# Recurrence and routed experts on one core: moving the tiles that TensorE reads to multiples of 64 bytes

## The chip, the core and the metric

The kernel runs on one core of a Trainium2 chip. A core has five engines with a queue each: TensorE (PE, with its weight loads as PEld), VectorE (DVE), ScalarE (ACT), GpSimd (POOL) and SyncE (SP, which issues most DMAs). The metric is the device time of one execution in microseconds; the median of several runs is compared.

## The reference

Two steps. First a linear recurrence over 768 time steps, for 4 batches and 8 heads of width 48:

```python
for t in range(S):
    cur = einsum('bhd,bhe->bhde', u * k[t], v[t])
    y[:, :, t] = einsum('bhd,bhde->bhe', r[t], state + cur)
    state = w[t][..., None] * state + einsum('bhd,bhe->bhde', k[t], v[t])
```

Then its output, as 3072 rows of 384 values, goes through a mixture of 8 experts. Each row is sent to the one expert with the largest logit (`x @ w_gate` plus a bias by the row's modality), and the result is

```python
out[mask] = gate_w[mask, None] * (np.maximum(x[mask] @ w1[e], 0) @ w2[e])
```

with 1024 hidden values per expert. Inputs and output are float32.

## The kernel before

**Recurrence** (`att_iter`, 24 chunks of 128 time steps). VectorE makes running products of the decays with two scans (tiles B and E, lines 286 and 289), VectorE and GpSimd form R = r * E, K = k * B and G = r * k, and TensorE does the chunk's matmuls in float32, which shows in the profile as two passes: the transpose of K (line 313), the scores (337), the bonus term with G (268), the state's update (351), and the output from state (363) and from scores (375, 378). The output rows go to `xp`, are transposed (419) and multiplied with the gate's weights (425). Routing then gives each row a place, and an indirect DMA per 128 rows (`scatter`, line 624) writes 386 values of each, the row, its weight and its number, to a buffer in DRAM sorted by expert.

**Experts**. Six blocks of up to 512 sorted rows (the last has 416), and one small block of 128. In a block, `rows_load` reads the rows, `blk_t` turns them and splits each value into a float32r part xh and a rest xo. `blk_up` computes 8 tiles of 128 hidden values, each as 9 matmuls: 3 slices of the row times the three products (wh, xh), (wh, xo) and (wl, xh), where wh and wl are the same split of w1 (line 692). The moving operand is xh or xo, 512 columns; the stationary one is a 128x128 piece of wh or wl. ScalarE and VectorE turn the sum into hh and hl, again such a split (lines 695 and 696). `blk_down` uses hh and hl as stationary operands and rows of w2's split as moving ones, 384 columns: 8 x 4 x 3 = 96 matmuls a block (line 706). The small block does its up-projection in plain float32 (line 737) and its down-projection like the others (line 750). For each expert ScalarE and GpSimd or VectorE split the next weights in slices (lines 219 and 220).

**What sets the order.** It is written by hand: the loops at the end of the function issue every instruction in its place, and each engine takes its own in that order. Waits between engines come from semaphores that the framework sets for tiles that are written and read.

**What sets the addresses.** Tiles come from pools, which lie in SBUF from the left side upwards (weights `raw`, `wh`, `wl`, small constants, `rt` with xp of the second part, `xa`, `wk`, and after the recurrence `wp` and `bp`) and from the right side downwards (`mp` with xl, xg, xh, xo, xt; `pa` with the recurrence's inputs; `hp` with hh and hl). A tile begins at the next multiple of 32 bytes in each partition. So a tile's place behind a multiple of 64 depends on the sizes of those before it.

The lines that the change touches are the tiles of lines 81, 283 and 284, 399, 642 and 643, and the reads at 234 and 625.

Of the kernel before, what the change touches and what calls it, by code (L numbers as in the profile page):

```python
# [9 lines left out]
F32 = mybir.dt.float32  # L10
# [4 lines left out]
ALU = mybir.AluOpType  # L15
AX = mybir.AxisListType

B, H, S, D = 4, 8, 768, 48
P = 128
# [4 lines left out]
E, F = 8, 1024  # L24
KC = DM // P
FC = F // P
XW = DM + 2
# [3 lines left out]
JT = BT // P  # L31
# [13 lines left out]
XROWS = DUMMY + BT  # L45
PAD_ID = 1 << 20
W_LO, W_HI = 0.78, 1.25
TINY = 1e-16
NWARM = 12
NG = 8  # L50
CUT = (0, 10, NU)
NJS = (CUT[1], NU - CUT[1])
GW = B * H * S * D // (P * NG)
WHALF = FC // 2 * DM
# [3 lines left out]
def kernel(ctx: ExitStack, tc: tile.TileContext, rkw, vt, wf, cst, mid, wg, bias, w1, w2, out):  # L58
    nc = tc.nc
    ctx.enter_context(tc.manual_schedule())  # L60
    cp = ctx.enter_context(tc.tile_pool(name="cp", bufs=1, side="left"))
# [2 lines left out]
    xs = dp.tile([XROWS, XW], F32, name="xs")  # L64


    raw = [cp.tile([P, FC, DM], F32, name=f"raw{k}") for k in range(2)]
    wh, wl = ([cp.tile([P, FC, DM], F32R, name=f"{nm}0")] for nm in ("wh", "wl"))

# [3 lines left out]
    rt = ctx.enter_context(tc.tile_pool(name="rt", bufs=2, side="left"))  # L73
    xa = att.enter_context(tc.tile_pool(name="xa", bufs=1, side="left"))
    wk = att.enter_context(tc.tile_pool(name="wk", bufs=2, side="left"))
    bp = {"m": ctx.enter_context(tc.tile_pool(name="mp", bufs=1, side="right"))}
    pa = prep.enter_context(tc.tile_pool(name="pa", bufs=2, side="right"))
    PREP = ("B", "E", "K", "G")
    WORK = ("R", "KT", "A", "dT", "v")
    NIN = 4  # L80
    ins = [pa.tile([P, 1541], F32, name=f"in{i}", bufs=1) for i in range(NIN)]
    T = {}

    def wt(n, tag, sh, bufs=None, dt=F32):
        T[tag, n] = (pa if tag in PREP else wk if tag in WORK else rt).tile(sh, dt, tag=tag, name=f"{tag}{n}", bufs=bufs)
        return T[tag, n]

    def pt(n, tag, sh=(P, 512)):
        T[tag, n] = banks.get(tag, ps).tile(list(sh), F32, tag=tag, name=f"{tag}_{n}")
        return T[tag, n]  # L90
# [31 lines left out]
    wp = pt("w", "pR")  # L122

    def warm(n):

        for i in range(n):
            nc.tensor.matmul(out=wp, lhsT=wm[:, 0:P], rhs=wm, start=(i == 0), stop=(i == n - 1))

    warm(NWARM)
    d1s = cp.tile([P, 518], BF16, name="d1s")  # L130
# [9 lines left out]
    bb = cp.tile([P, 2 * E], F32, name="bb")  # L140
    mi = cp.tile([NU, 2 * P], I32, name="mi")

    SPb = []
    for i in range(3):
        t = wk.tile([P, 4, 2, D], F32, name=f"SPb{i}", bufs=1)
        SPb.append(t)
    vz = [wk.tile([P, 2, 2, 2, D], F32, name=f"vz{i}", bufs=1) for i in range(2)]
    gacc = cp.tile([P, 2 * NG], F32, name="gacc")
    glo = cp.tile([P, 1], F32, name="glo")
# [81 lines left out]
        nc.scalar.copy(out=T["pX", a], in_=quarters(src))  # L231

    def mk_r(a):
        nc.vector.tensor_tensor(out=wt(a, "R", [P, 4, P], 3), in0=T["pX", a], in1=quarters(T["E", a])[:, :, 0:P], op=ALU.mult)

    def mk_k(a, k):
        nc.gpsimd.tensor_tensor(out=wt(a, "K", [P, 4, P]), in0=quarters(k), in1=quarters(T["B", a][:, 1:517])[:, :, 1:129], op=ALU.mult)  # L237
# [17 lines left out]
    def quarters(v):  # L255
        return v.rearrange("p (a b) -> p a b", a=4)
# [4 lines left out]
    def ok(n):  # L261
        return 0 <= n < NU
# [15 lines left out]
    def att_iter(i):  # L278
        a, m, z = i + 2, i + 1, i
        if ok(a):  # L280
            t = ins[a % NIN]
            r, k, w = t[:, 0:512], t[:, 512:1024], t[:, 1024:1541]
            Bt = wt(a, "B", [P, 517])
            Et = wt(a, "E", [P, 516], 1)

            nc.vector.tensor_tensor_scan(out=Bt[:, 516:0:-1], data0=w[:, 516:0:-1], data1=d1[:, 516:0:-1],  # L286
                                         initial=0.0, op0=ALU.mult, op1=ALU.max)
            nc.vector.reciprocal(out=w[:, 0:516:129], in_=Bt[:, 1:517:129])
            nc.vector.tensor_tensor_scan(out=Et, data0=w[:, 0:516], data1=d1[:, 1:2].to_broadcast([P, 516]),  # L289
                                         initial=1.0, op0=ALU.mult, op1=ALU.max)  # L290
        if ok(z):
            dV = wt(z, "dV", [P, H, D], 2)
            nc.gpsimd.tensor_tensor(out=dV, in0=T["v", z][:, 0:DM].rearrange("p (a b) -> p a b", a=H),
                                    in1=T["dT", z].rearrange("p a b -> p (a b)")[:, :, None].to_broadcast([P, H, D]), op=ALU.mult)
# [10 lines left out]
        if ok(m):  # L305
            K, R, v = T["K", m], T["R", m], T["v", m]

            if i == 0:
                warm(NWARM // 2)
            if not last:  # L310
# [10 lines left out]
        if ok(m):  # L321
            A = wt(m, "A", [P, 2, 2, 3, 64])
            pS = pt(m, "pS", (P, 2, 512))[:, :, 0:384].rearrange("p a (b c d) -> p a b c d", b=2, c=3)
            for g in range(2):
                for s0, c in ((0, 0), (1, 64)):
                    for sw in range(2):
                        for hh in range(2):
                            q = slice(64 * hh, 64 * hh + 64)
                            o = slice(64 * (s0 ^ sw), 64 * (s0 ^ sw) + 64)
                            p = 2 * g + sw  # L330
                            if s0:
                                out, rhs = pS[o, hh, g, 1 + sw], R[q, p, 64:P]
                            elif sw:
                                out, rhs = pS[o, hh, g, 0:3:2], R[q, p].rearrange("p (a b) -> p a b", a=2)
                            else:
                                out, rhs = pS[o, hh, g, 0:2], R[q, p].rearrange("p (a b) -> p a b", a=2)
# [21 lines left out]
        if ok(z):  # L358
            A, R, v, pY = T["A", z], T["R", z], T["v", z], pt(z, "pY")
# [35 lines left out]
    def x_rows(n, by_two=False):  # L395
        c, j = part(n)
        if j == 0:

            T["xp", c] = (rt if c else xa).tile([P, NJS[c], XW], F32, tag="xp", name=f"xp{c}", bufs=1)
        if n == 0:  # L400
            T["R"] = pt("x", "pR")

            nc.tensor.matmul(out=T["R"][:, 511:512], lhsT=wm[:, 0:P], rhs=wm[:, 0:1], start=True, stop=True, skip_group_check=True)
        x, dV = T["xp", c][:, j, 0:DM], T["dV", n].rearrange("p a b -> p (a b)")
        if by_two:
            nc.scalar.copy(out=x, in_=T["pY", n][:, 0:DM])
            nc.gpsimd.tensor_tensor(out=x, in0=x, in1=dV, op=ALU.add)
        else:
            nc.vector.tensor_tensor(out=x, in0=T["pY", n][:, 0:DM], in1=dV, op=ALU.add)

    def part(n):
        c = n >= CUT[1]
        return int(c), n - CUT[c]
# [208 lines left out]
    def scatter(n):  # L622
        b, j = part(n)
        rows_apart("xs", nc.gpsimd.indirect_dma_start(out=xs[:, :], out_offset=bass.IndirectOffsetOnAxis(ap=posT[:, n:n + 1], axis=0),  # L624
                                     in_=T["xp", b][:, j, :], in_offset=None, bounds_check=XROWS - 1, oob_is_err=False))


    X = {}
# [1 line left out]
    def width(q):  # L630
        return BQ if q == NQ - 1 else BT
# [8 lines left out]

    def rows_load(q, at, nj):
        xl = bp["m"].tile([P, NXB, XC], F32, tag="xl", name=f"xl{q}", bufs=2)
        xg = bp["m"].tile([P, JT, 2], F32, tag="xg", name=f"xg{q}", bufs=4)
        r = nc.sync.value_load(e0r[0:1, 0:1] if q == 0 else tab[0:1, 1, ds(at, 1)], min_val=0, max_val=DUMMY)
        src = xs[ds(r, nj * P), :]
        if q == 0:
            nc.sync.dma_start(out=xl.rearrange("p a c -> p (a c)").rearrange("p (j c) -> p j c", j=JT),
                              in_=src[:, 0:DM].rearrange("(j p) c -> p j c", p=P))
        for i in range(4 if q else 0):
            nc.sync.dma_start(out=xl[32 * i:32 * i + 32, 0:4 * nj], in_=src[:, XC * i:XC * i + XC].rearrange("(b t) c -> t b c", t=32))  # L650
        nc.sync.dma_start(out=xg[:, 0:nj], in_=src[:, DM:XW].rearrange("(j p) c -> p j c", p=P))
        X["xl", q], X["xg", q] = xl, xg
# [7 lines left out]
    def blk_t(q):  # L660
        w = width(q)
        X["x", q] = [bp["m"].tile([P, KC, BT], dt, tag=nm, name=f"{nm}{q}", bufs=1) for nm, dt in (("xh", F32R), ("xo", F32R), ("xt", F32))]
        xg = X["xg", q]
        xh, xo, xt = ([t[:, m, 0:w] for m in range(KC)] for t in X["x", q])
        if q == 0:
            xl = X["xl", q].rearrange("p a c -> p (a c)").rearrange("p (j k m) -> p j m k", j=JT, m=KC)
            xt = [pt(f"x0_{m}", t) for m, t in enumerate(("pX", "pK", "pU"))]
            for m in range(KC):
                for j in range(JT):
                    nc.tensor.transpose(out=xt[m][:, j * P:(j + 1) * P], in_=xl[:, j, m], identity=ident)  # L670

        def rest(m):
            nc.vector.tensor_tensor(out=xo[m], in0=xt[m], in1=xh[m].bitcast(F32), op=ALU.subtract)

        for m in range(KC):
            if q:
                rows_turn(q, m, w // 32, xt[m])
            nc.scalar.copy(out=xh[m], in_=xt[m])
            if m:
                rest(m - 1)  # L680
        rest(KC - 1)
        nc.vector.reciprocal(out=xg[:, :, 0:1], in_=xg[:, :, 0:1])
# [97 lines left out]
    for i in range(-2, NU):  # L780
# [39 lines left out]
        if i == NU - 3:  # L820
# [5 lines left out]
                                       in_=zt[:, None, :].to_broadcast([P, JT, XW])))  # L826
# [4 lines left out]
    banks.update(pS0=pse, pS1=pse)  # L831
    bp["h"] = ctx.enter_context(tc.tile_pool(name="hp", bufs=1, side="right"))
    wp = ctx.enter_context(tc.tile_pool(name="wp", bufs=1, side="left"))
    for w, nm in ((wh, "wh"), (wl, "wl")):
        w.append(wp.tile([P, FC, DM], F32R, name=f"{nm}1"))
    bp["p"] = ctx.enter_context(tc.tile_pool(name="bp", bufs=1, side="left"))
# [4 lines left out]
    def tend(s):  # L841
        for n in range(NG):
            if s == 26 + 6 * n:
# [218 lines left out]
def _layout(inp):  # L1062
# [14 lines left out]
    for hh in range(2):  # L1077
# [15 lines left out]
        "vt": vt,  # L1093
        "wf": np.ascontiguousarray(w).reshape(P, NG * GW),
        "cst": c,
# [19 lines left out]
```

## Time and profile before

| | us |
|---|---|
| median of 3 runs | 345.57 |
| their range | 343.74 to 351.85 |
| profiled execution | 348.94 |
| its span | 347.20 |

| engine | busy, us | share of the span | instructions |
|---|---|---|---|
| PE | 331.1 | 95% | 3950 |
| PEld | 297.7 | 86% | 3951 |
| DVE | 211.3 | 61% | 368 |
| ACT | 203.5 | 59% | 461 |
| POOL | 196.9 | 57% | 222 |

The mean granted clock of TensorE is 0.995 of full. Busy time counts a stretch once, however many instructions overlap in it; since the end of a matmul is modelled, its start tells more than its duration.

### The profile page before, as it was taken

What the parts mean: (1) busy time and instruction counts of PE and PEld (TensorE: products, weight loads), DVE (VectorE), ACT (ScalarE), POOL (GpSimd) and SP (SyncE); (2) the same over time, 40 slices, a digit from 0 to 9 for tenths busy, and PEclk for the clock granted to TensorE, in tenths of its full rate; (3) what the DMA queues carried; (4) which work ended last, traced back from release to release, by engine and by line L of the source; (5) the groups of instructions that cost most, each with busy time, mean ns of one, the idle gap of its engine ahead of it and who ended that gap; (6) DMA issues with size and microseconds to landing.
All of it is one profiled execution on the core that took longest, in us unless ns stands there. A gap on an engine that the chain in (4) does not pass through costs nothing. (4 is left out here: it accounts for less than half of the span.)

```text
span 347.2 us, 10131 instructions
## 1 busy us (share of the span) xinstructions
PE 331.1 (95%) x3950; PEld 297.7 (86%) x3951; DVE 211.3 (61%) x368; ACT 203.5 (59%) x461; POOL 196.9 (57%) x222
## 2 busy tenths in 40 slices
PE   7899989999999979999999999999999999999993
PEld 3789889988888867899889988997899889999893
DVE  6999989999998545776333955933560454053010
ACT  3897989778587735641522667628745855632140
POOL 8989898689998723586650680246024503440462
PEclk9999999999999989999999999999999999999999
DMA  7997988877997322515537047026544762260011
GB/s 258 408 354 232 293 275 240 275 251 248 278 312 231 111 72 93 91 68 197 216 119 156 0 96 226 0 70 144 197 159 160 208 223 93 92 206 3 0 47 55
DMA packets 35587, 58.66 MB, mean 169 GB/s; under 512 B 17298, under 2 KB 22090, under 8 KB 35529
## 3 DMA queue, kind: packets, MB, share of 16 engines
q1 hardware_dynamic: 32424, 48.45, 45.7%
q0 software_dynamic: 3104, 9.47, 7.6%
q8 instruction: 33, 0.54, 0.6%
q14 instruction: 26, 0.20, 0.2%
HBM read 57.86 MB, written 12.67 MB: 203 GB/s over the span
## 5 line engine op out<-in xcount | busy, mean ns | idle before, releaser
L220 POOL TENSOR_TENSOR wl<-raw,wh 128x768 fp32r<-128x768 f32 x24 | 46.3, 1935 | 106.8 <-ACT wh L219 106.7
L219 ACT CAST wh<-raw 128x768 fp32r<-128x768 f32 x48 | 39.3, 832 | 42.5 <-PE pU_d L706 39.0
L696 DVE SCALAR_TENSOR_TENSOR hl<-pS_u,hh 128x512 fp32r<-128x512 f32 (+1 forms) x34 | 22.8, 675 | 44.0 <-ACT hh L695 44.0
L692 PE MATMUL pS_u<-xh,wh 128*128 128x512 f32 (+1 forms) x102 | 40.5, 397 | 0.4 <-DVE hl L696 0.4
L692 PE MATMUL pS_u<-xo,wh 128*128 128x512 f32 (+1 forms) x102 | 39.6, 389 | 0.0
L692 PE MATMUL pS_u<-xh,wl 128*128 128x512 f32 (+1 forms) x102 | 39.6, 388 | 0.0
L695 ACT ACTIVATE hh<-pS_u 128x512 fp32r<-128x512 f32 (+1 forms) x34 | 19.7, 586 | 33.0 <-PE pS_u L692 27.7
L237 POOL TENSOR_TENSOR K<-in,B 128x512 f32<-128x512 f32 x24 | 28.4, 1185 | 7.2 <-issue 2.7
L297 POOL TENSOR_TENSOR G<-in 128x512 f32<-128x512 f32 x24 | 30.8, 1284 | 0.0
L624 POOL DMA_INDIRECT xs<-xp,posT x24 | 26.2, 1092 | 7.3 <-issue 5.1
L286 DVE TENSOR_TENSOR_SCAN B<-in,pX_d 128x516 f32<-128x516 f32 x24 | 29.3, 1219 | 1.6 <-DMA in<-rkw 1.6
L220 DVE TENSOR_TENSOR wl<-raw,wh 128x768 fp32r<-128x768 f32 x24 | 27.2, 1141 | 4.9 <-ACT wh L219 4.6
L289 DVE TENSOR_TENSOR_SCAN E<-in,pX_d 128x516 f32<-128x516 f32 x24 | 29.5, 1229 | 0.8
L715 POOL DMA_INDIRECT out<-ot,xg x24 | 23.5, 979 | 9.1 <-issue 4.1
L378 PE MATMUL pY<-v,A 128*64 128x48 f32 x384 | 27.2, 225 | 1.3 <-issue 1.3
L378 PEld LDWEIGHTS pY<-v,A 128*64 128x64 f32 x384 | 25.7, 142 | 1.4 <-issue 1.4
L339 DVE TENSOR_TENSOR A<-pS,m 128x768 f32<-128x768 f32 x24 | 22.8, 949 | 3.3 <-PE pS L337 3.0
L696 DVE SCALAR_TENSOR_TENSOR hl<-pT_u,hh 128x512 fp32r<-128x512 f32 (+1 forms) x14 | 9.4, 668 | 25.3 <-ACT hh L695 25.3
L243 ACT ACTIVATE pU_st<-pU_st,B 128x48 f32<-128x48 f32 x80 | 22.0, 275 | 2.9 <-PE pU_st L351 0.5
L692 PEld LDWEIGHTS pS_u<-xh,wh 128*128 128x128 f32 x102 | 19.2, 188 | 4.5 <-DVE hl L696 0.8
L692 PEld LDWEIGHTS pS_u<-xh,wl 128*128 128x128 f32 x102 | 19.1, 188 | 4.2
L692 PEld LDWEIGHTS pS_u<-xo,wh 128*128 128x128 f32 x102 | 19.2, 188 | 3.6
(232 smaller groups left out, 911.3 us busy)
## 6 DMA issues: line engine op xcount, KB each, us to landing
raw<-w SPq DMA_DIRECT2D x24, 768.0 KB
in<-rkw SPq DMA_DIRECT2D x23, 512.0 KB
v<-vt SPq DMA_DIRECT2D x24, 288.0 KB
in<-rkw SPq DMA_DIRECT2D x23, 258.5 KB
wg<-wf SPq DMA_DIRECT2D x8, 576.0 KB
xl<-xs SPq DMA_DIRECT2D x20, 192.0 KB
raw<-w SPq DMA_DIRECT2D x16, 192.0 KB
xs<-zt SPq DMA_DIRECT2D x12, 193.0 KB
```

Source lines behind the costliest of these rows:

```text
L219: nc.scalar.copy(out=wh[k][:, sl], in_=raw[k][:, sl])
L220: (eng or (nc.vector, nc.gpsimd)[k]).tensor_tensor(out=wl[k][:, sl], in0=raw[k][:, sl], in1=wh[k][:, sl].bitcast(F32), op=ALU.subtract)
L237: nc.gpsimd.tensor_tensor(out=wt(a, "K", [P, 4, P]), in0=quarters(k), in1=quarters(T["B", a][:, 1:517])[:, :, 1:129], op=ALU.mult)
L286: nc.vector.tensor_tensor_scan(out=Bt[:, 516:0:-1], data0=w[:, 516:0:-1], data1=d1[:, 516:0:-1], initial=0.0, op0=ALU.mult, op1=ALU.max)
L289: nc.vector.tensor_tensor_scan(out=Et, data0=w[:, 0:516], data1=d1[:, 1:2].to_broadcast([P, 516]), initial=1.0, op0=ALU.mult, op1=ALU.max)
L297: nc.gpsimd.tensor_tensor(out=wt(a, "G", [P, 512]), in0=r, in1=k, op=ALU.mult)
L339: nc.vector.tensor_tensor(out=fl(A), in0=fl(pS), in1=m3.rearrange("p c d -> p (c d)")[:, None, None, :].to_broadcast([P, 2, 2, 192]), op=A ...
L378: nc.tensor.matmul(out=yh[64:P, g, sw, hh], lhsT=A[:, hh, g, 1 + sw], rhs=vs[:, g, hh] if sw else v[:, h * D:(h + 1) * D], start=new and n ...
L624: rows_apart("xs", nc.gpsimd.indirect_dma_start(out=xs[:, :], out_offset=bass.IndirectOffsetOnAxis(ap=posT[:, n:n + 1], axis=0), in_=T["xp ...
L692: nc.tensor.matmul(out=pp, lhsT=wsrc[0][:, f, c * P:(c + 1) * P], rhs=xsrc[:, c], start=(n == 0), stop=(n == 3 * KC - 1))
L696: nc.vector.scalar_tensor_tensor(out=hl, in0=pp, scalar=0.0, in1=hh.bitcast(F32), op0=ALU.max, op1=ALU.subtract)
L715: ins = nc.gpsimd.indirect_dma_start(out=out[:, :], out_offset=bass.IndirectOffsetOnAxis(ap=xg[0:n, j, 1:2].bitcast(I32), axis=0), in_=ot[ ...
```

## The change

It adds four tiles that nothing reads or writes (`pad0` to `pad3`) and makes some rows longer than what is used of them: the input tiles have 1600 values a row instead of 1541, B and E 576 instead of 517 and 516, xp 400 instead of 386, xg 4 instead of 2. What is read and written of each tile is as before, and so is every instruction and its place on its engine.

```diff
+PADW, PADK = 48, 80
...
+    cp.tile([P, 32], F32, name="pad0")
     raw = [cp.tile([P, FC, DM], F32, name=f"raw{k}") for k in range(2)]
...
-    ins = [pa.tile([P, 1541], F32, name=f"in{i}", bufs=1) for i in range(NIN)]
+    ins = [pa.tile([P, 1600], F32, name=f"in{i}", bufs=1) for i in range(NIN)]
...
+    wk.tile([P, PADK], F32, name="pad3", bufs=1)
     SPb = []
...
-        nc.vector.tensor_tensor(out=wt(a, "R", [P, 4, P], 3), in0=T["pX", a], in1=quarters(T["E", a])[:, :, 0:P], op=ALU.mult)
+        nc.vector.tensor_tensor(out=wt(a, "R", [P, 4, P], 3), in0=T["pX", a], in1=quarters(T["E", a][:, 0:516])[:, :, 0:P], op=ALU.mult)
...
-            Bt = wt(a, "B", [P, 517])
-            Et = wt(a, "E", [P, 516], 1)
+            Bt = wt(a, "B", [P, 576])
+            Et = wt(a, "E", [P, 576], 1)[:, 0:516]
...
-            T["xp", c] = (rt if c else xa).tile([P, NJS[c], XW], F32, tag="xp", name=f"xp{c}", bufs=1)
+            T["xp", c] = (rt if c else xa).tile([P, NJS[c], 400], F32, tag="xp", name=f"xp{c}", bufs=1)
...
-                                     in_=T["xp", b][:, j, :], in_offset=None, bounds_check=XROWS - 1, oob_is_err=False))
+                                     in_=T["xp", b][:, j, 0:XW], in_offset=None, bounds_check=XROWS - 1, oob_is_err=False))
...
-        xg = bp["m"].tile([P, JT, 2], F32, tag="xg", name=f"xg{q}", bufs=4)
+        xg = bp["m"].tile([P, JT, 4], F32, tag="xg", name=f"xg{q}", bufs=4)[:, :, 0:2]
...
+        if q == 0:
+            bp["m"].tile([P, 56], F32, name="pad1")
...
     wp = ctx.enter_context(tc.tile_pool(name="wp", bufs=1, side="left"))
+    wp.tile([P, PADW], F32, name="pad2")
```

Where the tiles begin in the two built programs, in bytes within a partition, and what is left over a multiple of 64 (in the last column over one of 256):

| tile | read by TensorE as | before | left over 64 | after | left over 64 | over 256 |
|---|---|---|---|---|---|---|
| xh, xo | moving, line 692 | 210912, 217056 | 32 | 210688, 216832 | 0 | 0 |
| wh, wl of w1 | stationary, line 692 | 26752, 39040 | 0 | 26880, 39168 | 0 | 0 |
| hh (first) | stationary, lines 706, 750 | 165728 | 32 | 165376 | 0 | 0 |
| hl (first) | stationary, lines 706, 750 | 182112 | 32 | 181760 | 0 | 0 |
| wh, wl of w2 | moving, lines 706, 750 | 92096, 104384 | 0 | 93184, 105472 | 0 | 0 |
| xq, raw of w1 | moving, stationary, line 737 | 134336, 2176 | 0 | 135424, 2304 | 0 | 0 |
| K, G (first) | stationary, lines 313, 337, 268 | 190304, 194400 | 32 | 189952, 194048 | 0 | 0 |
| R, KT, A, v, vz, SPb (all) | both sides of 337 to 378 | | 32 | | 0 | |
| xp, row j | stationary, line 419 | 92096 + 1544 j | 8 j | 92992 + 1600 j | 0 | |
| xT | stationary, line 425 | 66048 | 0 | 66176 | 0 | |
| wm (bf16) | both, line 127 | 51328 | 0 | 51456 | 0 | 0 |
| identity | moving, lines 313 and 419 | 52352 | 0 | 52480 | 0 | 0 |

Slices that TensorE takes inside these tiles begin a multiple of 64 bytes further on (but for the gate's weights, whose second of three slices begins 32 bytes off in both, and xl of the first block, read with a step). Of the inputs' four tiles the first and third began at a multiple before and the others 32 bytes off; now all four do. Small bf16 constants of the routing (`onesb`, `trib`) stay 32 bytes off.

## Rows read from the trace of the kernel before

**Rows 1.** Busy time by stage: length; per engine busy (instructions); clock; DMA share; GB/s.

```profile
core 0: us, PE busy (x) PEld busy (x) DVE busy (x) ACT busy (x) POOL busy (x), PEclk, DMA share, GB/s
20.00:133.00 113.00, 106.41 (x2557) 97.27 (x2556) 99.51 (x161) 84.98 (x254) 89.34 (x101) 0.98 0.74 235
133.00:165.40 32.40, 32.40 (x197) 28.98 (x197) 21.82 (x57) 14.12 (x23) 20.78 (x27) 1.00 0.43 125
...
233.00:267.30 34.30, 33.89 (x169) 30.26 (x168) 13.25 (x19) 21.91 (x35) 11.29 (x8) 1.00 0.54 165
...
301.00:341.60 40.60, 40.60 (x243) 38.26 (x241) 8.62 (x27) 13.09 (x23) 16.94 (x13) 1.00 0.20 62
```

**Rows 2.** Waits from 133 to 342 us: who for whom, total us, times, longest.

```profile
POOL wl L220 <- ACT wh L219: 106.7, 20, 16.1
DVE hl L696 <- ACT hh L695: 69.2, 40, 13.4
...
PEld pS_u L692 <- DVE hl L696: 0.8, 1, 0.8
```

**Rows 3.** Timeline of PE, third block: start us, length us, instruction, count.

```profile
199.17 0.40 PE L692 MATMUL pS_u<-xh,wh 128*128 128x512 f32 x1
199.41 0.39 PE L692 MATMUL pS_u<-xo,wh 128*128 128x512 f32 x1
199.64 0.39 PE L692 MATMUL pS_u<-xh,wl 128*128 128x512 f32 x1
199.87 0.40 PE L692 MATMUL pS_u<-xh,wh 128*128 128x512 f32 x1
...
215.74 0.39 PE L692 MATMUL pT_u<-xh,wl 128*128 128x512 f32 x1
215.97 0.34 PE L706 MATMUL pY_d<-wh,hh 128*128 128x384 f32 x1
...
232.75 0.34 PE L706 MATMUL pU_d<-wh,hl 128*128 128x384 f32 x1
```

**Rows 4.** Timeline of PE, last block's up-projection, six steps apart.

```profile
302.65 0.35 PE L692 MATMUL pS_u<-xh,wl 128*128 128x416 f32 x1
...
303.81 0.35 PE L692 MATMUL pT_u<-xh,wl 128*128 128x416 f32 x1
```

**Rows 5.** Timeline of PE, the second warm-up in bf16 and what follows.

```profile
10.36 1.24 PE L127 MATMUL pR_w<-wm 128*128 128x512 bf16 x5 [0.16 <-issue]
11.44 0.38 PE L313 MATMUL pK<-cs,K 128*128 128x128 f32 x2
```

**Rows 6.** Line views: duration ns min/median/max, first and last start, shapes (L750: x8).

```profile
L692 PE MATMUL pS_u<-xh,wl x102: 345/394/399, 129.5 to 313.2; 128*128 128x512 f32 x87, 128*128 128x416 f32 x15
L692 PE MATMUL pT_u<-xh,wl x42: 347/392/399, 165.9 to 314.9; 128*128 128x512 f32 x33, 128*128 128x416 f32 x9
L706 PE MATMUL pY_d<-wh,hh x48: 337/337/341, 148.5 to 329.9; 128*128 128x384 f32 x48
L750 PE MATMUL pX_d<-wh,hh x8: 337/338/425, 337.3 to 341.1; 128*128 128x384 f32 x8
```

**Rows 7.** Timeline of PE in the recurrence: short matmuls.

```profile
60.45 0.63 PE L268 MATMUL pT<-cs,G 128*64 128x2 f32 x16
60.91 0.53 PE L425 MATMUL pR_x<-cs,xT 128*64 128x8 f32 x12
61.26 0.31 PE L363 MATMUL pY<-SPb,R 128*64 128x96 f32 x2
```

**Rows 8.** Line views: duration ns min/median/max of 128 columns with 128x128 stationary.

```profile
L419 PE MATMUL pT<-cs,xp x63: 272/273/331, 20.5 to 116.8; 128*128 128x128 f32 x63
L313 PE MATMUL pK<-cs,K x80: 272/273/329, 7.2 to 112.2; 128*128 128x128 f32 x80
L737 PE MATMUL pS_u<-xq,raw x48: 273/275/275, 332.0 to 337.3; 128*128 128x128 f32 x48
```

**Rows 9.** Line view of VectorE's first scan.

```profile
L286 DVE TENSOR_TENSOR_SCAN B<-in,pX_d x24: 1216/1218/1229, 3.6 to 110.5; 128x516 f32<-128x516 f32 x24
```

**Rows 10.** DMA issues: count, KB each, or us to landing where no size stands.

```profile
xs<-xp,posT POOLq DMA_INDIRECT x24, 3.6
...
xg<-xs SPq DMA_DIRECT2D x6, 4.0 KB
```

**Rows 11.** Timeline of PE, last block's down-projection, fourth tile of 32 rows.

```profile
320.94 0.34 PE L706 MATMUL pU_d<-wh,hh 128*32 128x384 f32 x1
321.11 0.34 PE L706 MATMUL pU_d<-wl,hh 128*32 128x384 f32 x1
321.28 0.34 PE L706 MATMUL pU_d<-wh,hl 128*32 128x384 f32 x1
321.46 0.34 PE L706 MATMUL pY_d<-wh,hh 128*128 128x384 f32 x1
```

## The prediction, made before the changed kernel ran

> **What bounds the kernel now.** I read the busy time by stage first. The program has two halves. Up to about 133 us runs the recurrence, and there VectorE is busy 99.5 of 113 us and TensorE 106.4 by overlapping records: neither has a stage for itself. From 133 to 341.6 us run six expert blocks and one small block, and TensorE is busy in every microsecond of each stage but 0.4 us of one, while VectorE, ScalarE and GpSimd have a third or more of their time free [rows 1]. The granted clock is 1.00 there, the higher level of 2.4 GHz. The list of waits in that half says the same from the other side: the long ones are ScalarE, VectorE and GpSimd waiting for each other or for TensorE, and the longest wait on TensorE's side, its weight loads' for VectorE, is 0.8 us in all [rows 2]. So in 208 us a nanosecond more or less per matmul arrives at the end unchanged, and what else the change moves has cover.
>
> Next the question how long a matmul takes there. Its recorded duration contains a modelled end, so I take the spacing of starts. An up-projection runs from 199.17 to 215.74 us with 72 matmuls of 512 columns: 71 steps in 16.57 us, 233.4 ns each. The down-projection behind it starts at 215.97 and its last matmul at 232.75: 95 steps, 176.6 ns each for 384 columns [rows 3]. In the block of 416 columns six steps take 1.16 us, 193.3 ns each [rows 4]. At 2.4 GHz these are the times of 560, 424 and 464 columns: 48, 40 and 48 more than are computed. The only other full-rate stream is the warm-up in bf16, 512 columns, both operands at a multiple of 64 bytes: five steps from 10.36 to 11.44 us, 216 ns or 518 columns, 6 more [rows 5].
>
> So every float32r matmul of the second half pays for 34 to 42 columns more than the bf16 ones do. In the up-projections the moving operand (xh, xo) begins at 32 bytes past a multiple of 64 and the weights at a multiple. In the down-projections it is the other way round: the stationary operand (hh, hl) is off and the moving weights are not. The change puts all of them on a multiple.
>
> **Part by part.** *Nothing is removed, added or reordered*: every engine has the same instructions in the same order, with the same shapes; only addresses differ. What can change is the duration of an instruction, so I go by kind.
>
> *Up-projections, moving operand*: three products in two sets of banks, (87 + 33) x 3 = 360 matmuls of 512 columns and (15 + 9) x 3 = 72 of 416 [rows 6]. The bounds are 0 ns (the address does not count) and 233.4 - 216 = 17.4 ns (all that is over the bf16 warm-up). The nearest row is the down-projection, whose moving operand is already on a multiple: its excess is 40 columns against 48, which is 8 columns, 3.3 ns. It has another fault, though, and starts in the up-projection do not wander: they come 0.24, 0.23, 0.23 us apart, in a fixed pattern of three [rows 3]. I take 16 columns, 6.7 ns, since 512 values that begin in mid-stretch lie in 33 stretches of 64 bytes, and on a multiple in 32. This is an estimate: one stretch of 16 values at 2.4 GHz. 432 x 6.7 ns = 2.9 us.
>
> *Down-projections, stationary operand*: three products into four tiles, 12 x 48 = 576 matmuls, and 3 x 8 = 24 of the small block [rows 6], 600 in all. Upper bound: 384 columns at 2.4 GHz with the bf16 warm-up's excess of 2.7 ns are 162.7 ns, against 176.6: 13.9 ns. Lower bound 0. Two places speak for 0. Sixteen short matmuls whose stationary operand (G) begins 32 bytes off start at 60.45 us and the next kind at 60.91: 28.8 ns each. Twelve whose stationary operand (xT) is on a multiple, with the same 64 columns of weights, go from 60.91 to 61.26: 29.2 ns each [rows 7]. And the transposes of routed rows have eight different beginnings (the row of 1544 bytes moves each by 8 bytes) and yet their shortest and their median duration are 272 and 273 ns, the same as those of K, 32 bytes off, and not above the small block's matmuls with both operands on a multiple, 275 ns [rows 8]. The last are the nearest in shape (128 columns of weights), so I take 0. That these streams are slower per column than a float32r one is why the upper bound stays in the range.
>
> *Recurrence* (R, K, KT, A, G, v, vz, SPb, xp): the comparisons just made are from there and show nothing, so 0. VectorE's scans read inputs that begin on a multiple in every second chunk and 32 bytes off in the others, and all 24 take 1216 to 1229 ns [rows 9]: longer rows of `ins`, B and E cost or give nothing. If TensorE did gain there, VectorE's 88% of the stage would take up most of it.
>
> *Scatter and row loads*: the indirect DMA reads the same 1544 bytes of a row now 1600 bytes apart and takes 3.6 us to land off TensorE's path; xg's rows of four values instead of two are small [rows 10]. Cost 0: the scatters of the second part lie under the 208 us of matmuls. Without that cover they would still move the same bytes in the same number of pieces.
>
> **Sum.** -2.9 us. The profiled execution took 348.94 us, 347.2 of span and 1.7 around it, so it would become 346.0. It is 3.4 us above the median of the three runs, 345.57, and I count from the median: **342.7 us**, 0.8% less. A measurement of this kernel tells about 2% from no change: its three runs alone differ by 2.4%.
>
> **Rivals.**
>
> *All the excess goes.* If float32r at full rate has no cost of its own and any operand off a multiple breaks the stream, up drops by 17.4 ns and 17.3 ns (416 columns: 193.3 against 176.0), down by 13.9: 360 x 17.4 + 72 x 17.3 + 600 x 13.9 ns = 15.8 us, giving 329.8. For it: the bf16 stream, both operands on a multiple, and each slow stream has exactly one operand off. Against it: two different faults would have to cost nearly the same, and a bf16 value is half as wide. [...] Chance 0.27.
>
> *One stretch for each operand.* Down gains 6.7 ns too: 1032 x 6.7 = 6.9 us, giving 338.7, at the edge of 2%. The last block's down-projection loads 32 columns of weights in the fourth tile and still starts every 0.17 to 0.18 us [rows 11], so a stationary cost would have to be independent of its length. Chance 0.13.
>
> *It does nothing for time.* 32 bytes may be as good a beginning as 64, and the excess be float32r's own: 345.6 us. For it: every comparison in the recurrence. [...] Chance 0.25.
>
> *Slower.* Now both reads of a pair begin at the same place of every 64 bytes (in the second half of 256), where they were 32 apart. If they then meet in the memory, each of 1032 pairs could wait one stretch more: 6.9 us, 352.5, slower by 2%. It decides from 6.7 ns a pair. For it: the one stream with both operands on a multiple is 2 ns longer than the transposes [rows 8]; against it, 2 ns are 0.6%, and bf16 pairs read the same tile without harm. Chance 0.05.
>
> **Numbers.** The forecast has 0.30. Its own range is 340.7 (3.3 ns for down too) to 345.6. Both better cases together hold 0.40, so the range must reach them: 328.5 to 347, the upper end from no gain plus some spread of runs, leaving out the slower case and the tails. Faster by over 2%: 0.27 and half of 0.13, 0.33. Within 2%: 0.62. Slower: 0.05.
>
> **What would show it.** The spacing in the profile after: 226.7 ns for 512 columns and 176.6 still for 384 is my case; 216 and 163 the first rival, 227 and 170 the second, 233 and 177 the third, 240 and 183 the last. Durations of the recurrence's matmuls, of the scans and of the scatter should not move. I am wrong if the down-projection's spacing falls, for then a stationary beginning counts at full rate though it did not in the short streams; or if TensorE starts to wait for `wl` or `hl`, which would mean that its pace hid another bound.

## The result and the profile after

| | before | after |
|---|---|---|
| median of six runs, us | 346.25 (343.74 to 351.85) | 342.46 (341.94 to 343.37) |
| profiled execution / span, us | 348.94 / 347.2 | 342.68 / 340.9 |

The ratio is 0.9883, with a 95% interval of [0.9844, 0.9923]: 1.2% less; the medians differ by 3.8 us. The ratio is taken over fast runs alone, leaving out executions over 1.5% above the fastest of their kernel, here the one of 351.85 us. The time lies where the prediction put it, inside "within 2%". But only part of its reason held, as the spacing of starts shows. This is the timeline of PE in the third expert block of the kernel after (start us, length us, instruction); it answers to [rows 3], and line 692 is now 697, 706 is 711:

```profile
195.42 0.39 PE L697 MATMUL pS_u<-xh,wh 128*128 128x512 f32 x1
195.65 0.40 PE L697 MATMUL pS_u<-xo,wh 128*128 128x512 f32 x1
...
203.39 0.39 PE L697 MATMUL pS_u<-xh,wl 128*128 128x512 f32 x1
...
211.55 0.39 PE L697 MATMUL pT_u<-xh,wl 128*128 128x512 f32 x1
211.78 0.33 PE L711 MATMUL pY_d<-wh,hh 128*128 128x384 f32 x1
...
228.27 0.33 PE L711 MATMUL pU_d<-wh,hl 128*128 128x384 f32 x1
```

The 71 steps of the up-projection take 16.13 us, 227.2 ns each instead of 233.4. The 95 of the down-projection take 16.49 us, 173.6 instead of 176.6. From here on "pace" means this quotient, worked out from starts to the nanosecond. Three of the full blocks (first, second, fourth) hold waits in some runs; their pace is that of their longest stretch without one, 26 to 54 matmuls. The lengths at two decimals hardly moved; in the line views their medians fell as the paces did, from 394 to 389 ns for (xh, wl) and from 337 to 334 ns for (wh, hh).

The pace holds a slower beginning of each block. From 203.39 to 211.55 us, 36 steps, it is 226.7 ns. A column costs 0.417 ns in these streams: the steady spacing before grows by 40.0 ns from 416 to 512 columns (193.3 to 233.3), that of after by 53.4 from 384 to 512 (173.3 to 226.7). That is the 2.4 GHz of the prediction, 2.4 columns a ns at a granted clock of 1.00; the lower level in the trace before is 0.50, from 126 to 128 us, ahead of the experts. So 226.7 ns are the time of 544 columns: 32 more than the 512 that are computed. The same stretch took 233.3 ns before, 48 columns more. In the down-projections the steady spacing is 173.3 ns, again 32 columns more than are computed, against 176.7, 40 more. So in the full blocks the change took away 16 columns a matmul in one stream and 8 in the other, and left 32 in both.

The sum over the program, pace by pace: 360 up-projections x 6.1 ns and 72 of 416 columns x 4.6 ns (194.7 before, 190.2 after) are 2.5 us; down-projections of five blocks, 480 x 3.0 ns, are 1.45 us; the sixth block's are still at 176.0 (176.1 before). Together 4.0 us, against 3.8 in the medians. (The small block's 24, 3.4 ns faster each, add under 0.1 us.)

The two spans differ by 6.3 us, more than that. 3.6 us of it lie ahead of the first expert matmul, which starts at 128.91 us before and at 125.28 after. Nothing lays that part to the places of the tiles: the first expert matmul starts anywhere from 123.6 to 127.3 us in the eleven profiles below, whatever stood on which address, and the kernel before with only its weights moved (`e_before_w`) starts it at 123.90. 1.3 us of it is the wait for the first rows to be read (2.1 us before, 0.8 after); what made up the rest was not followed. From the first to the last expert matmul it is 212.5 us before and 210.0 after, and after has in it one stall of 1.2 us that before had not, seen in the second block's timeline (without it, in the second profile `e_after`, the stretch is 208.8 us, 3.7 less than before):

```profile
173.28 0.39 PE L697 MATMUL pS_u<-xh,wl 128*128 128x512 f32 x1
174.50 0.50 PE L697 MATMUL pT_u<-xh,wh 128*128 128x512 f32 x1 [0.82 <-DVE hl L701]
```

The list of waits of after from 128 to 336 us (who for whom: total us, times, longest):

```profile
POOL wl L223 <- ACT wh L222: 99.7, 20, 15.1
DVE hl L701 <- ACT hh L700: 61.8, 31, 13.0
...
PEld pT_u L697 <- DVE hl L701: 1.2, 1, 1.2
...
PEld pS_u L697 <- issue: 1.0, 1, 1.0
...
PE pT_u L697 <- DVE hl L701: 0.8, 1, 0.8
...
PE pS_u L697 <- issue: 0.5, 1, 0.5
```

TensorE's side waits for `hl` once, in the second block (PE and PEld list the same stall). This stall comes at either pace, in `e_x_off` at 233.3 ns and in `e_before_w` at 227.0, and is missing at either, in the kernel before and in `e_after`; so the faster pace uncovered no new bound. The wait of [rows 2], in the fourth block, is still there, listed as "issue": the step between two starts is 0.93 us where it was 0.80. The first block, which has waits too, is 0.26 us shorter where 71 steps at the two paces make 0.43. Together this takes back 0.3 of the 4.0 us, and 3.7 is what `e_after` shows. The busy time by stage of after reads as [rows 1] (columns as there; the stages lie a little earlier):

```profile
core 0: us, PE busy (x) PEld busy (x) DVE busy (x) ACT busy (x) POOL busy (x), PEclk, DMA share, GB/s
20.00:133.00 113.00, 108.51 (x2586) 98.59 (x2585) 101.48 (x163) 87.34 (x260) 91.11 (x102) 1.00 0.76 239
133.00:165.40 32.40, 32.40 (x189) 29.34 (x189) 21.53 (x56) 15.04 (x25) 21.22 (x28) 1.00 0.44 139
199.20:233.00 33.80, 33.80 (x173) 30.82 (x172) 18.73 (x40) 20.47 (x33) 12.68 (x10) 1.00 0.34 100
```

What was not to move did not: transposes, K, the small block's matmuls and the scans have the durations of [rows 8, 9], and the matmuls' starts are as far apart as before (medians of 109 to 110 ns for transposes and K, 112 for the small block). For the scatter the trace after gives no time to landing. The line views (ns min/median/max):

```profile
L422 PE MATMUL pT<-cs,xp x63: 272/273/332, 20.6 to 115.4; 128*128 128x128 f32 x63
L316 PE MATMUL pK<-cs,K x80: 272/273/333, 7.3 to 110.5; 128*128 128x128 f32 x80
L742 PE MATMUL pS_u<-xq,raw x48: 271/275/276, 325.9 to 331.1; 128*128 128x128 f32 x48
L289 DVE TENSOR_TENSOR_SCAN B<-in,pX_d x24: 1216/1218/1229, 3.6 to 108.6; 128x516 f32<-128x516 f32 x24
```

### The profile page after: what moved, and what is told of

Read it like the earlier page. It is cut to its first block, busy times and chain, and to the rows that moved or that the text cites. A ratio compares the mean times of both kernels' runs of the same rounds, so it can differ in the third digit from the quotient of the medians.

```text
span 340.9 us, 10132 instructions
## 1 busy us (share of the span) xinstructions
PE 326.5 (96%) x3951; PEld 294.5 (86%) x3951; DVE 210.9 (62%) x368; ACT 203.2 (60%) x461; POOL 197.8 (58%) x222
## 5 line engine op out<-in xcount | busy, mean ns | idle before, releaser
L720 POOL DMA_INDIRECT out<-ot,xg x24 | 24.5, 1021 | 9.1 <-issue 4.4
L381 PE MATMUL pY<-v,A 128*64 128x48 f32 x384 | 26.3, 222 | 0.0
L381 PEld LDWEIGHTS pY<-v,A 128*64 128x64 f32 x384 | 24.8, 138 | 0.1
```

Source lines behind the costliest of these rows:

```text
L381: nc.tensor.matmul(out=yh[64:P, g, sw, hh], lhsT=A[:, hh, g, 1 + sw], rhs=vs[:, g, hh] if sw else v[:, h * D:(h + 1) * D], start=new and n ...
L720: ins = nc.gpsimd.indirect_dma_start(out=out[:, :], out_offset=bass.IndirectOffsetOnAxis(ap=xg[0:n, j, 1:2].bitcast(I32), axis=0), in_=ot[ ...
```

## The experiments

They came in two steps: first which tiles give the gain, then which property of their addresses. `e_sweep`, `e_w_off` and `e_sweep2` ran once each, for their paces; the others have intervals. "Up" is the pace for 512 columns, "down" that for 384.

### Which tiles: inputs, hidden rows, recurrence

`e_x_off`: the changed kernel with xh and xo (moving, up) 32 bytes higher, off a multiple of 64 again.

```
+        if q == 0:
+            bp["m"].tile([P, 8], F32, name="pad4")
         X["x", q] = [bp["m"].tile(...)]
...
-            bp["m"].tile([P, 56], F32, name="pad1")
+            bp["m"].tile([P, 48], F32, name="pad1")
```

> The changed kernel with xh and xo alone 32 bytes past a multiple of 64, as before; hh, hl and the recurrence stay on a multiple. Theory of one stretch per misaligned operand: up-projections start every 233.4 ns again (227.2 in the changed kernel), down-projections stay at 173.6; the time rises by 432 x 6.1 ns = 2.6 us over the changed kernel's 342.5, to 345.1. Rival, that most of the gain comes from the recurrence: spacing changes, but the time stays under 343.5.

Measured: 345.07 us, ratio to before 0.9964 [0.9936, 0.9993]; up 233.3, down 173.4 to 173.6. The up-projections' gain is gone and the down-projections' is there.

`e_h_off`: instead hh and hl (stationary, down) 32 bytes lower.

```
+        if q == 0 and f == 0:
+            bp["h"].tile([P, 8], F32, name="pad5")
```

> The changed kernel with hh and hl alone 32 bytes off. Theory: down-projections of the first five blocks go from 173.6 back to 176.6 ns, up-projections stay at 227.2; 480 x 3.0 ns = 1.4 us more than 342.5: 343.9. If the stationary operand's place does not count at full rate and the down-projection's gain came from elsewhere, 173.6 stays and the time too.

Measured: 344.31 us, 0.9941 [0.9912, 0.9970]; up 227.24, down 176.65 in all five full blocks. So each gain belongs to its own tile.

`e_xh_off`: both edits.

> The changed kernel with xh, xo, hh and hl 32 bytes off: only the recurrence has the change. Theory: 233.4 and 176.6 ns, 2.6 + 1.4 us over 342.5: 346.5, as slow as the kernel before (346.2). Rival recurrence: under 344, and the first expert matmul still starts 3 to 4 us earlier than in the profile of the kernel before (125.3 against 128.9 us).

Measured: 344.66 us, 0.9956 [0.9926, 0.9986]. Up is 233.3. Down is 176.7 in the first, second and fifth block and 173.4 in the third and fourth, with the same addresses. The timeline of its second and third block's down-projections, first and last matmul (16.78 and 16.47 us for 95 steps):

```profile
179.25 0.34 PE L715 MATMUL pY_d<-wh,hh 128*128 128x384 f32 x1
...
196.03 0.33 PE L715 MATMUL pU_d<-wh,hl 128*128 128x384 f32 x1
...
213.00 0.34 PE L715 MATMUL pY_d<-wh,hh 128*128 128x384 f32 x1
...
229.47 0.34 PE L715 MATMUL pU_d<-wh,hl 128*128 128x384 f32 x1
```

A stream can thus settle into one of two paces and keep it to its end. That is why this kernel keeps some of the gain: two blocks x 96 x 3.3 ns are 0.6 us, the last block 0.5 more (190.7 ns in its up- and 174.2 in its down-projection, against 194.7 and 176.1 before).

`e_rec_off`: the changed kernel with the recurrence's tiles and its input tiles (`ins`) 32 bytes off.

```
-PADW, PADK = 48, 80
+PADW, PADK = 48, 88
...
+            if a == 0:
+                pa.tile([P, 8], F32, name="pad6", bufs=1)
```

> The changed kernel with the recurrence's operands 32 bytes off as before (SPb, vz, v, R, KT, A, K, G, and the inputs, B and E with them); experts as changed. Theory: nothing in the recurrence depends on it, 342.5 within 0.7, first expert matmul at about 125.3 us unless a stall falls into it. Rival recurrence: 3 us slower, 345.5, first expert matmul at about 128.9 us.

Measured: 343.26 us, 0.9923 [0.9881, 0.9965]; up 227.24, down 173.61, and the first expert matmul starts at 124.17 us, earlier than in the changed kernel. The pads of the recurrence give nothing that can be seen: the paces are those of the changed kernel, and the two intervals overlap. The times alone would leave room for a loss of 1 to 2 us; a second pair, `e_xh_off` and `e_all_off` below, where the recurrence's places are the only difference, is 0.1% apart in its ratios.

`e_all_off`: the changed kernel with its pads and long rows, but xh and xo, hh and hl, and the recurrence all 32 bytes off; `e_after`: the changed kernel again, beside it.

> The changed kernel with its pads and long rows, but with xh, xo, hh, hl and all operands of the recurrence 32 bytes past a multiple of 64 again. Theory, that the places and nothing else make the difference: the time of the kernel before, ratio 1.00 within 0.4%, 4.0 us over the changed kernel; 233.3 ns in up-projections, 176.6 in down-projections unless they fall into the faster pace of 173.4 that two of them showed with the same places. Rival, that row lengths or the scatter's source rows give part of it: about 0.996, as the kernel with only xh and hh off.

> The changed kernel once more, beside the next one and runs of the kernel before. Theory: ratio to the kernel before about 0.988, spacing 227.2 and 173.6 ns, first expert matmul where a stall of the recurrence happens to put it. If the expert blocks alone make the gain, it is 2.6 + 1.4 = 4.0 us below the next kernel.

Measured: `e_all_off` 344.22 us, 0.9968 [0.9935, 1.0]; `e_after` 341.43 us, 0.9885 [0.9846, 0.9924], with the paces of the changed kernel. In `e_all_off` up is 233.3; down is 176.7 in three blocks and 173.4 in two, the last block a little faster (174.2, and 190.6 for its 416 columns where before had 194.7). By these paces 1.1 us of the gain should remain, and 1.1 (0 to 2.2) do.

### Which property: a multiple of 64, or the distance between the operands

The multiples of 64 had changed together with something else. Over 256 bytes (by what their beginnings leave over a multiple of 256) the moving and the stationary operand began 96 (up: xh at 224, wh at 128) and 96 (down: wh at 192, hh at 96) apart before; after, all begin at 0 and the distance is 0. In `e_x_off` it is 32 for up, in `e_h_off` 32 for down, since hh and hl lie 32 bytes lower there. Theories: *multiple* (each operand for itself has to begin on a multiple of 64) and *distance* (only the difference counts).

`e_sweep`: xh, xo, hh and hl have 256 bytes longer rows and are used from byte 16, 8, 48, 64 and 4 on in the five full blocks; weights at 0.

```
+OX = {0: 4, 1: 2, 2: 12, 3: 16, 4: 1}
+OH = {0: 4, 1: 2, 2: 12, 3: 16, 4: 1}
```

> The changed kernel with rows of xh, xo, hh, hl longer by 256 bytes, and used in blocks 0 to 4 from byte 16, 8, 48, 64 and 4 on (the last block from 0). Theory of stretches of 64 bytes: block 3 (64) runs at 227.2 and 173.6 ns, all others near 233.4 and, for the stationary operand, 173.4 or 176.6. If lines of 16 bytes count, blocks 0, 2 and 3 are fast and 1 and 4 slow. If multiples of 256 count, block 3 is slow too.

Measured: up 231.6, 233.5, 233.2, 229.0 and 236.8 in that order; down 173.5, 173.5, 173.5, 173.4 and 175.0 (343.21 us in one run). Even 64, a multiple, is 1.8 ns slower than 0, and 4 bytes are worse than the kernel before.

`e_w_off`: all weights 32 bytes off; xh, xo, hh, hl from byte 0, 32, 16, 0, 32 and 32 on.

```
-PADW, PADK = 48, 80
+PADW, PADK = 56, 80
+OX = {0: 0, 1: 8, 2: 4, 3: 0, 4: 8, 5: 8}
...
+    cp.tile([P, 8], F32, name="pad7")
     ...
+    cp.tile([P, 56], F32, name="pad8")
```

> The changed kernel with the split weights wh and wl 32 bytes off, which are stationary in the up- and moving in the down-projection; xh, xo, hh, hl used in blocks 0 to 5 from byte 0, 32, 16, 0, 32, 32 on. If the moving operand's place costs 16 columns and the stationary one's 8 on average, up-projections run at 230 ns in blocks 0 and 3 (moving on a multiple, stationary off) and at 233 to 237 in 1, 2, 4; down-projections at 180 everywhere or a little above. If only the distance between the two operands counts, blocks 1 and 4 with both 32 bytes off run as in the changed kernel, at 227.2 and 173.6.

The timeline of its second block (both operands at 32) and the third's up-projection (16 against 32):

```profile
163.83 0.39 PE L702 MATMUL pT_u<-xh,wh 128*128 128x512 f32 x1
...
179.97 0.39 PE L702 MATMUL pS_u<-xh,wl 128*128 128x512 f32 x1
180.19 0.33 PE L716 MATMUL pY_d<-wh,hh 128*128 128x384 f32 x1
...
196.69 0.33 PE L716 MATMUL pU_d<-wh,hl 128*128 128x384 f32 x1
196.86 0.40 PE L702 MATMUL pS_u<-xh,wh 128*128 128x512 f32 x1
...
213.63 0.40 PE L702 MATMUL pT_u<-xh,wl 128*128 128x512 f32 x1
```

With both 32 off, 16.14 and 16.50 us: the changed kernel's 227.2 and 173.6 ns without one operand on a multiple of 64. With 16 against 32 the third block needs 16.77 us, 236.1 ns. The first and fourth block, xh on a multiple and the weights 32 off, take 233.2 and 233.1. For the up-projections of full blocks distance decides, in one kernel, from block to block. The down-projections of the first and fourth block have one distance (32) and the same addresses, and take 176.7 and 173.3: there distance alone does not decide.

`e_before_w`: the kernel *before*, all its long and short rows as they were, with four pads that move the weights alone, so that both operands of a pair begin at 224 (up) or 96 (down) over 256.

```
+    cp.tile([P, 24], F32, name="pad1")
     ... wh, wl of w1
+    cp.tile([P, 40], F32, name="pad2")
...
+    wp.tile([P, 40], F32, name="pad3")
     ... wh, wl of w2
+    wp.tile([P, 24], F32, name="pad4")
```

> The kernel before with four pads of its own and nothing else: the split weights of w1 move up by 96 bytes, those of w2 by 160, everything else keeps its place over a multiple of 256. Now both operands of every float32r matmul begin 32 bytes past a multiple of 64 and none on a multiple. Theory of the distance (a matmul is fast when its two operands begin at the same place): 227.2 and 173.6 ns, ratio to the kernel before 0.988 like the changed kernel. Theory of multiples of 64: at best nothing is gained, 233 and 177 ns, ratio 1.00; with both operands off, slower.

Measured: 343.28 us, 0.9898 [0.9858, 0.9938]. Its third block:

```profile
194.14 0.39 PE L694 MATMUL pS_u<-xh,wh 128*128 128x512 f32 x1
...
210.26 0.40 PE L694 MATMUL pT_u<-xh,wl 128*128 128x512 f32 x1
210.49 0.34 PE L708 MATMUL pY_d<-wh,hh 128*128 128x384 f32 x1
...
226.99 0.34 PE L708 MATMUL pU_d<-wh,hl 128*128 128x384 f32 x1
```

227.0 and 173.7 ns: the whole gain, with every operand of these streams 32 bytes off a multiple of 64.

`e_mult64`, the opposite: the changed kernel with xh, xo moved up by 128 bytes and hh, hl down by 128. All stay on multiples of 64 (of 128 even); the distance is 128.

```
+            bp["m"].tile([P, 32], F32, name="pad4")
...
-            bp["m"].tile([P, 56], F32, name="pad1")
+            bp["m"].tile([P, 24], F32, name="pad1")
...
+            bp["h"].tile([P, 32], F32, name="pad5")
```

> The changed kernel with xh and xo 128 bytes higher and hh and hl 128 bytes lower: every operand that it moved still begins on a multiple of 64 (and of 128), but the two operands of a float32r matmul are 128 bytes apart over a multiple of 256. Theory of the distance over 256 bytes: the up-projections run near 232.4 ns and the down-projections near 176 as in the sweep's block with 128, and 432 x 5.2 + 480 x 2.4 ns = 3.4 us of the gain is lost: ratio to the kernel before 0.998. Theory of multiples of 64: the gain stays, 227.2 and 173.6 ns, ratio 0.988.

Measured: 346.22 us, 0.9953 [0.9914, 0.9991]. Its third block:

```profile
197.70 0.39 PE L699 MATMUL pS_u<-xh,wh 128*128 128x512 f32 x1
...
214.20 0.40 PE L699 MATMUL pT_u<-xh,wl 128*128 128x512 f32 x1
214.44 0.34 PE L715 MATMUL pY_d<-wh,hh 128*128 128x384 f32 x1
...
231.16 0.34 PE L715 MATMUL pU_d<-wh,hl 128*128 128x384 f32 x1
```

232.4 and 176.0 ns. *Multiple* asked for 0.988, which lies outside the interval; *distance* for 0.998, inside. The two kernels together settle it for this kernel's gain: multiples of 64 are neither needed nor enough.

`e_sweep2`: as `e_sweep`, from byte 96, 128, 192, 64 and 224.

> The changed kernel with xh, xo, hh, hl used in blocks 0 to 4 from byte 96, 128, 192, 64 and 224 on (the last block from 0), the weights on a multiple of 256. If only the distance modulo 64 counts: blocks 1, 2, 3 (128, 192, 64) fast, near 227.2, and 0 and 4 (96, 224) near 233.3. Distance 64 gave 229.0 in the first sweep, 1.8 ns over 0; if a longer period counts a little, 128 lies between or at 227.2, and 64 shows 229.0 again.

Measured: up 233.4, 232.4, 233.2, 229.0 and 233.2; down 173.4, 176.0, 173.3, 173.4 and 173.3 (344.07 us in one run). 96 repeats the kernel before to 0.1 ns, 128 repeats `e_mult64`.

All paces of the five full blocks by distance (moving minus stationary, over 256 bytes), ns:

| distance | up, 512 columns | down, 384 columns |
|---|---|---|
| 0 | 227.0 to 227.3 | 173.4 to 173.7 |
| 4 | 236.8 | |
| 8 | 233.5 | |
| 16 | 231.6 | 176.6 |
| 32 | 233.3 | 176.7 (12 blocks) or 173.3 to 173.4 (6) |
| 48 | 233.2 | |
| 64 | 229.0 | 173.3 |
| 96 | 233.4 | 176.6 |
| 128 | 232.4 | 176.0 |
| 160 | | 173.4 |
| 192 | 233.2 | 173.4 |
| 208 | | 173.5 |
| 224 | 233.2 | |
| 240 | 236.1 | 173.5 |
| 248, 252 | | 173.5, 175.0 |

The column on the right says less than the one on the left. For 512 columns only distance 0 reaches 227 ns. For 384 columns the fast pace comes at most distances that were tried (64, 160, 192, 208, 240, 248), and the slow one only at 16, 96 and sometimes 32, with 128 and 252 between them; most of these have one block in one run, so a second pace may have been missed.

The last block, with 416 columns and a narrower fourth tile, does not follow the table. Its up-projection needs 194.7 ns at distance 96, but 189.2 to 190.2 at 0, 189.8 at 128 and 190.6 to 190.7 at 32; its down-projection needs 176.1 at 96, 175.9 to 176.2 at 0, 175.1 at 128 and 174.2 at 32, the fastest. At 32 the up-projection changes its pace half-way, in all three kernels that have it. In `e_x_off`:

```profile
298.66 0.35 PE L699 MATMUL pS_u<-xh,wl 128*128 128x416 f32 x1
...
302.14 0.34 PE L699 MATMUL pS_u<-xh,wl 128*128 128x416 f32 x1
...
303.95 0.35 PE L699 MATMUL pS_u<-xh,wl 128*128 128x416 f32 x1
...
310.67 0.35 PE L699 MATMUL pT_u<-xh,wl 128*128 128x416 f32 x1
```

The 18 steps up to 302.14 are of 193.3 ns, 48 columns more than are computed. After two longer steps (225 and 272 ns, from 302.14 on) the 36 from 303.95 are of 186.7 ns, 32 more, at the same addresses. At distance 0 the second half goes at 188.3 in the changed kernel and at 186.7 in `e_before_w`, described above. So the addresses alone do not settle the pace: 193.3 and 186.7 ns stand at the same ones, and what sets which was not shown.

## Why the prediction came out in time and not in its reason

*The time*: 342.5 us against 342.7 is closer than the working was, and that is luck. The change took off 3.8 us where 2.9 were added up. The missing part is the down-projections', and the median of the kernel before, from which the forecast counted, had moved from 345.57 to 346.25.

*What bounds the kernel*: right. The second half is TensorE's, and 4.0 us of shorter pace arrive as 3.8 us in the medians. "Unchanged" was a little too much: 0.3 us went into waits of the first and fourth block.

*Up-projections, moving operand*: the size was right, 6.1 ns a matmul against the 6.7 taken, 2.5 us against 2.9; in the steady part of a full block it is the 16 columns themselves, 233.3 to 226.7 ns. The reason, "512 values that begin in mid-stretch lie in 33 stretches of 64 bytes", fell: in `e_w_off` and `e_before_w` they begin in mid-stretch and go at 227 ns, in `e_mult64` they begin on a multiple and go at 232.4. That one stretch is 6.7 ns was a coincidence of size: other distances gain 4.4 ns (64) or lose 3.4 (4).

*Down-projections, stationary operand*: this is the step that failed. "The last are the nearest in shape (128 columns of weights), so I take 0": measured 3.0 ns, 480 x 3.0 = 1.45 us, in five of six blocks. The comparison itself was sound, since transposes and K still take 273 ns after the change; but they stream 128 columns, and what was to be judged streams 384. The trace of before had no stream of 384 columns at another distance, so the row that would have shown the 3.0 ns was missing. The case's own test, "226.7 ns for 512 columns and 176.6 still for 384", failed in its second half. What the prediction gave for that, "for then a stationary beginning counts at full rate", holds with one addition: it counts against the moving operand's beginning, not by itself (hh at 96 over 256 goes at 176.6 ns with the weights at 192, at 173.7 with them at 96).

The last block's down-projection kept 176.0 ns. Its fourth tile still has 32 columns, and around it the starts are unevenly spaced, as the timeline of after shows (0.18, 0.17, 0.17, 0.18, 0.17 and 0.19 us apart):

```profile
319.04 0.34 PE L711 MATMUL pU_d<-wh,hh 128*32 128x384 f32 x1
319.22 0.34 PE L711 MATMUL pU_d<-wl,hh 128*32 128x384 f32 x1
319.39 0.33 PE L711 MATMUL pU_d<-wh,hl 128*32 128x384 f32 x1
319.56 0.34 PE L711 MATMUL pY_d<-wh,hh 128*128 128x384 f32 x1
319.74 0.34 PE L711 MATMUL pY_d<-wl,hh 128*128 128x384 f32 x1
319.91 0.35 PE L711 MATMUL pY_d<-wh,hl 128*128 128x384 f32 x1
320.10 0.34 PE L711 MATMUL pX_d<-wh,hh 128*128 128x384 f32 x1
```

The narrow tile alone is not the reason: with it, the same block goes at 174.2 in `e_h_off`, `e_xh_off` and `e_all_off`, at distance 32. Why distance 0 does not help there is open.

*Recurrence, longer rows at 0*: nothing speaks against it (`e_rec_off`; scans of 1218 ns in both; `e_all_off`, where the paces explain what the long rows and pads still gain). *Scatter at 0*: no run shows its time after the change.

*The rivals*. "All the excess goes" is excluded: at distance 0 13.9 ns (227.2 over 213.3 for 512 columns of 0.417 ns) stay, 11.2 ns more than the bf16 warm-up's 2.7; in the steady part of the full blocks 32 columns stay at both widths. "One stretch for each operand" asked for 170 ns in the down-projections, and they gained less than half of that. "Does nothing" is excluded by the interval. "Slower" named the right quantity, the place of both reads relative to each other, and had its sign wrong for the full blocks: at the same place 512 columns go fastest, and 384 as fast as anywhere.

What stays open: why the pace depends on where the two operands begin relative to each other. The runs show that it does, with 227.0 to 236.8 ns for one and the same instruction of 512 columns, and no row shows by what. What leads a down-projection at distance 32 to 176.7 in one block and 173.4 in the next is open too, and so are the last block's other order and the 32 columns that remain.

No version beats the changed kernel. `e_before_w` reaches the same (0.9898 and 0.9885, intervals overlapping) with four pads on the weights.

## What to carry to other kernels

When TensorE alone sets the pace, read it as the spacing of starts over a whole stream, to a tenth of a nanosecond, and compare it with the columns; a recorded length contains a modelled end. When a change aligns several things at once, test the property that it did not name: moving one side by a pad (the weights alone) and moving both by the same amount tells "aligned" from "aligned to each other". A rule found on one width has to be tried on another: here it held for 512 columns, in part for 384, and not for 416. And a cost of zero taken from short instructions says nothing of long ones of the same kind: here 128 columns stayed at 273 ns, and 384 went from 176.6 to 173.6.

## What the runs showed of the hardware

- A float32r matmul stream of 512 columns whose weights change at every matmul has a pace that depends on the distance between the beginnings of its two operands over 256 bytes: 227.0 to 236.8 ns, both operands at 0, 32 or 224 over 256 being equally fast (227.0 to 227.3). In `e_before_w` the up-projection's operands are 256 apart over 512 bytes, and it goes at 227.0 ns against 227.2 in the changed kernel, where they are 0 apart.
- The worst distance seen was 4 bytes (236.8 ns), next that of 240 (236.1): the inputs 16 bytes short of the weights' place.
- The steady spacing of these streams was 32, 40 or 48 columns above those computed in most blocks: 226.7 and 233.3 ns for 512 columns, 173.3 and 176.7 for 384, 186.7 and 193.3 for 416. No block of 512 or 384 columns went below 32.
- A stream at one set of addresses can have either of two paces. For 384 columns at distance 32 a block held 173.4 or 176.7 ns from its first matmuls to its last; for 416 columns at distance 32 the stream went from 193.3 to 186.7 ns after two longer steps. At distance 0 every full block of 384 held 173.4 to 173.7.
- The transposes of routed rows and of K and the small block's matmuls (128 columns) kept medians of 273 and 275 ns, with the recurrence's tiles on a multiple or 32 bytes off, and with the weights moved.
